# A linear-attention and two-layer kernel: the rows of its two split heads moved by four transfers instead of twelve

## The chip, the core and the metric

The kernel runs on one core of a Trainium2 chip. A core has a matrix engine (TensorE, PE in the profile, with its weight loads as PEld), three engines for elementwise work (VectorE or DVE, ScalarE or ACT, GpSimd or POOL), and a queue (SyncE, SP) on which this kernel issues all its transfers to 16 DMA engines. Each engine works through its own list of instructions in order and waits at an instruction until what it needs is there. The metric is the device time of one execution in microseconds (us); less is better.

## The reference

Gated linear attention over 4 batches, 8 heads, 768 steps and 48 features a head, then two feed-forward layers over the 3072 tokens (`d_model` 384, `d_ff` 2048 and 1536):

```python
state = np.zeros((B, H, D, D))
for t in range(S):
    state = alpha[:, :, t, :, None] * state + einsum('bhd,bhe->bhde', k[:, :, t], v[:, :, t])
    y[:, :, t] = einsum('bhd,bhde->bhe', q[:, :, t], state)
x = y.transpose(0, 2, 1, 3).reshape(B * S, H * D)
h = x @ w_in;  x = (h * np.cos(h)) @ w_out          # first layer
out = ((x @ w_a) * (x @ w_b)) @ w_out2              # second layer
```

## The kernel before

**Units.** The attention is cut into 48 units of 64 steps (12 for each batch). A unit has its input (`in_t`, for the first eight units `w_t`), two scans on DVE over the gates (L288, L300, with a reciprocal L297 between), products with queries and keys on POOL or DVE (L312, L325), a transpose and the scores on PE (L358, L368, L371), a copy of the transposed keys on ACT (`kn`, L363), the masked scores on DVE (`m`, L397 or L404), the new state and the outputs on PE (L430 to L450), and the state's decay (L499, or L514 and L517). The outputs of a unit leave PSUM twice: ACT rounds them (L547), DVE takes the rest that the rounding left (L550). These two, hi and lo, are the first layer's input, so that three products of rounded numbers stand for one product of full ones.

**The layer's input.** A group is 512 tokens, or eight units. Its input is two tiles, `xhi_t` and `xlo_t`, of 128 partitions x 4 slots x 512 columns. A unit writes partitions 0 to 47 (an even head) and 64 to 111 (an odd head) of all four slots. The layer reads only slots 0 to 2, as three blocks of 128 features; so heads 6 and 7, which stand in slot 3, have to come to the free partitions 48 to 63 and 112 to 127 of the slots 0 to 2. Once for every four units (12 times in all) SP issues transfers inside SBUF that do this: `move`, L563 to L573. The order of the rows of `w_in` (`perm`, L1084) follows from where the rows go.

**The layers.** A step of the first layer is nine 128x512 products into `hp` (L647), a cosine made by ACT and DVE in turn (L697, L700, L705), the product with `h` (L708), its rounding and rest (L712, L716), and nine products into `acc` (L654). There are 16 steps for each of 6 groups. For the first group the first two steps are done in halves of 256 columns: the first half needs the first move (units 0 to 3), the second half the second move (units 4 to 7). The second layer has 12 steps for each group (`ap`, `bp`, `acc`).

**Weights** come as 64-bit floats: 34 transfers `st_t<-wts` (L586) of 768 KB into three buffers. ACT scales the upper word (L590) and, for the first 16, makes the lower bits (L595; later L597 on DVE), DVE puts the bits together (L601, L607; the last of them frees the buffer for a later transfer), ACT rounds (L616), POOL takes the rest (L627).

**The order.** Every piece of work above is given to `Plan` with an engine, a duration in us, a lag (time from its end until others see it), what it needs and sometimes a due time. `Plan.run` simulates the five engines with these numbers and emits the instructions in the order in which that simulation starts them. So a duration in such a call changes no instruction, but can change the order on every engine. Around the place of the change:

```python
ops["ld"] = op(SP, 1.75, load, lag=2.0)      # a unit's input
mv = op(SP, 0.8, move, E["yx", k4], lag=2.0) # the transfers of four units
ld = op(SP, 2.4, load, after, lag=2.0)       # a weight pair
us = ou = op(PE, 2.0 + (0.8 if carry else 0.0), block, ...)
```

Of the kernel before, what the change touches and what calls it, by code (L numbers as in the profile page):

```python
# [28 lines left out]
P = 128  # L29
# [137 lines left out]
def chunked(ctx: ExitStack, tc: tile.TileContext, u_in: bass.AP, wts: bass.AP, out: bass.AP, in_range: bass.AP):  # L167
# [86 lines left out]

    def xtile(g):
        if g not in xg:
            xg[g] = tuple(xpool.tile([P, NP, G], F32R, name=f"x{n}_t") for n in ("hi", "lo"))
        return xg[g]

    def plan_load(u):  # L260
        d, ops = un[u], U[u]
        if "ld" in ops:
            return ops["ld"]
        def load():
            if u < UG:
                t = wpool.tile([P, 2, 2 * DM], F32R, name="w_t").bitcast(F32)
                d["in"] = t.rearrange("p a c -> p (a c)")[:, 0:IN_COLS]
            else:
                d["in"] = att.tile([P, IN_COLS], F32, name="in_t", bufs=NIN)
            cuts = (0, NA + 1, IN_COLS) if u == 0 else (0, IN_COLS)  # L270
            for c0, c1 in zip(cuts, cuts[1:]):
                nc.sync.dma_start(out=d["in"][:, c0:c1], in_=u_in[u, :, c0:c1])  # L272

        ops["ld"] = op(SP, 1.75, load, lag=2.0)
        ops["in_last"] = take("w_t", NPAIR1, ops["ld"]) if u < UG else take("in", NIN, ops["ld"])
        return ops["ld"]

    def plan_front(u):
        d, ops = un[u], U[u]
        apart = u < APART  # L280
        due = unit_due(u)

        ld, in_last = plan_load(u), U[u]["in_last"]

        def scan_a():
            d["ar"] = att.tile([112, 2, NP, SEP], F32, name="ar_t", bufs=NAR)
            d["a"], d["r"] = d["ar"][:, 0], d["ar"][:, 1]
            nc.vector.tensor_tensor_scan(  # L288
                d["a"].rearrange("p c t -> p (c t)"), d["in"][0:112, 0:NA], first.rearrange("p c t -> p (c t)"), 0.0,
                op0=ALU.mult, op1=ALU.add,  # L290
            )

        sa = op(DVE, 0.7, scan_a, [ld], port=True)
        ar_last = take("ar", NAR, sa)

        def recip():
            nc.vector.reciprocal(last[:, :, C:SEP], d["a"][:, :, C:SEP])  # L297

        def scan_r():
            nc.vector.tensor_tensor_scan(  # L300
                d["r"].rearrange("p c t -> p (c t)")[:, ::-1], d["in"][0:112, NA:0:-1],
                last.rearrange("p c t -> p (c t)")[:, ::-1], 0.0, op0=ALU.mult, op1=ALU.add,
            )

        rc = op(DVE, 0.18, recip, [sa, U[u - 1]["sr"] if u else None])
        sr = ops["sr"] = op(DVE, 0.7, scan_r, [rc], port=True)
        m = m_t[u % 3]
        m_before = U[u - 3]["ou"] if u >= 3 else []
        ma = [
            op(  # L310
                POOL, 0.73,
                lambda rows=rows, i=i: nc.gpsimd.tensor_tensor(  # L312
                    m[rows, i + apart], part(u, 0)[rows], d["a"][rows, :, 1:], op=ALU.mult
                ),
                [sa, *m_before], port=True,
            )
            for rows, i in HEADS
        ]
        kt = k_t[u % 2]
        k_before = U[u - 2]["k_last"] if u >= 2 else []  # L320
        on = DVE if u < UG else POOL
        eng = nc.vector if on == DVE else nc.gpsimd
        k = [op(
            on, 0.45 if on == DVE else 0.75,
            lambda: eng.tensor_tensor(kt, d["r"][:, :, 1:], part(u, 1), op=ALU.mult), [sr, *k_before], port=True,  # L325
        )]

        def in_range_sum():
            nc.scalar.activation(  # L329
                d["in"][0:112, W_A - 2 * NA:W_A], d["ar"].rearrange("p a c t -> p (a c t)"), AF.Square,  # L330
                accum_out=ranges[:, u:u + 1],
            )

        rg = op(ACT, 0.82, in_range_sum, [sr, *ma, *k], due=due + 2.0)
        E.setdefault("ranges", []).append(rg)
        in_last += [rg]
        ar_last += [rg, *ma, *k]

        ops.update(k=k, ma=ma, in_last=in_last, ar_last=ar_last, m_before=m_before)
# [4 lines left out]
    def plan_scores(u, block=None):  # L344
# [44 lines left out]
        ops["emit"] = ([transpose] if state else []) + [score]  # L389
        ops["k_last"] = [sc]  # L390
        if state:
            ops["kn"] = kn = op(ACT, 0.36, copy_k, [sc, *(U[u - 2]["us_op"] if u >= 2 else [])])
            ops["tu"] += [kn]
        if apart:
            mk = [op(
# [18 lines left out]
    def plan_back(u):  # L414
# [56 lines left out]
        else:  # L471
# [9 lines left out]
                if state and carry:  # L481
                    old_state()

            us = ou = op(PE, 2.0 + (0.8 if carry else 0.0), block, [kn, ld, *mk, *ma, *before], due=due)
            tu_last, sy_last = take("tu", 1, us), take("sy", 1, us)
            ops["us_op"] = [us]
            if u + 1 < NU:
# [64 lines left out]
                op0=ALU.mult, op1=ALU.subtract,  # L552
            )

        xh = op(ACT, 0.46, hi, [ou])
        if off == 0:
            E["xl", g] = take("x", 2, xh)
            E["xfirst", g] = xh
        need(xh, E["xfirst", g] if off else None)
        xl = op(DVE, 0.44, lo, [xh])  # L560
        sy_last += [xh, xl]
        E.setdefault(("yx", k4), []).extend([xh, xl])
        if off4 == UB - 1:  # L563
            def move():
                xc = slice((k4 % 2) * XB, (k4 % 2 + 1) * XB)
                xs = [t.bitcast(F32) for t in xg[g]]
                for n in range(2):
                    for r0 in (0, 64):
                        for j in range(KT):
                            nc.sync.dma_start(  # L570
                                out=xs[n][r0 + 48:r0 + 64, j, xc], in_=xs[n][r0 + 16 * j:r0 + 16 * j + 16, 3, xc]
                            )

            mv = op(SP, 0.8, move, E["yx", k4], lag=2.0)
            E["x", k4] = [mv, *E["yx", k4]]


# [5 lines left out]
    def plan_weights(i, after=(), gate=None):  # L583
# [42 lines left out]
            t = split.pop(i)  # L626
            nc.gpsimd.tensor_tensor(t[:, 1], conv.pop(i), t[:, 0].bitcast(F32), op=ALU.subtract)  # L627

        ld = op(SP, 2.4, load, after, lag=2.0)
        st_last = take("stage", NST, ld)  # L630
        s = op(ACT, 0.92, scale, [ld])
        wf_last = take("wf", 2, s)
# [2 lines left out]
        b1 = op(DVE, 0.93, bits1, [b0], port=True)  # L635
        h = op(ACT, 0.84, hi, [b1, gate])
        w_last = [] if NPAIR1 <= i < NPAIR1 + NLATE else take("w_t", NPAIR1, h)
        o = op(POOL, 1.95, lo, [h], port=True)
        st_last += [s, l, b0, b1]
        wf_last += [b0, b1, h, o]  # L640
        W[i] = dict(ld=ld, b1=b1, hi=h, lo=o, last=w_last)
# [25 lines left out]
    def plan_step(g, f):  # L667
# [3 lines left out]

        def mm():
            s["u"] = bank("hp", "hp", 3)
            by_k(s["u"], w1s[f, 0], *xg[g])

        def mm_part(n):
            def fn():
                if n == 0:
                    s["u"] = bank("hp", "hp", 3)
                by_k(s["u"][:, n * XB:(n + 1) * XB], w1s[f, 0], *(t[:, :, n * XB:(n + 1) * XB] for t in xg[g]))  # L680
            return fn

        w = [W[f]["hi"], W[f]["lo"]]
# [73 lines left out]
    def plan_x2(g):  # L757
# [4 lines left out]
        for j in range(KT):  # L762
            def hi(j=j):
                if j == 0:
                    x2s[g] = tuple(xpool.tile([P, NP, G], F32R, name=f"x{m}_t") for m in ("hi", "lo"))
                nc.scalar.copy(x2s[g][0][:, j, :], x2[g][:, j, :])  # L766

            def lo(j=j):
# [152 lines left out]
def step_by_step(  # L921
# [76 lines left out]
    with tc.For_i(0, NG, 1) as g:  # L998
        cols = bass.ds(g * G, G)
        x = pool.tile([P, KT, G], F32, name="g_x", bufs=1)  # L1000
        for j in range(KT):
            for r0, f0, n in (
                (0, 2 * j * D, D), (48, 6 * D + 16 * j, 16), (64, (2 * j + 1) * D, D), (112, 7 * D + 16 * j, 16)
            ):
                nc.sync.dma_start(out=x[r0:r0 + n, j, :], in_=y_all[f0:f0 + n, cols])
        nc.vector.tensor_scalar(x, x, XS, None, op0=ALU.mult)
        accs = [bank(f"g_acc{j}") for j in range(KT)]
        for f in range(NF1):
# [104 lines left out]
```

## Time and profile before

| | |
|---|---|
| time, median of 3 runs | 996.8 us (994.27 to 997.29) |
| profiled execution | 997.82 us, of it the span of the trace 996.0 us |
| PE busy | 975.5 us (98%), 6909 matrix products |
| PEld, DVE, ACT, POOL busy | 799.5, 524.9, 407.8, 227.7 us |
| mean granted clock of PE | 0.988 of full speed |
| chain that ended last | PE 90%, DMA 3%, SPq 2%, ACT 2%, DVE 1% |

The span is what lies between the first and the last instruction of the trace. Times of rows are counted from its start. "SPq" is the time in which SP issues transfers; what the transfers themselves take is told separately as the time to landing. A granted clock of 1.00 is 2.4 GHz and of 0.50 is 1.2 GHz; a mean between them says for how much of a stretch each was granted. An idle time stands in square brackets behind the instruction that ended it, with what released it.

### The profile page before, as it was taken

Reading aid. Unit: us, or ns where it says so; the run is one execution under the profiler, and the core shown is the slowest. Engines: PE = TensorE matmul, PEld = TensorE weight load, DVE = VectorE, ACT = ScalarE, POOL = GpSimd, SP = SyncE. Lnnn points to the kernel's source line nnn. Section 1 sums busy time; section 2 is a strip of 40 time slices with the busy share of each in tenths; the row PEclk is TensorE's granted clock in tenths of the full one; section 3 lists DMA queues with packets and bytes.
Section 4 is the critical chain, followed back from the end, with each engine's and each line's share of the span. In section 5 each row is a group of like instructions: output and inputs, shape, how many; then the busy total and the mean of one; then the engine's idle time right before and its main releaser. Section 6 shows DMA issues by size and latency. Waiting matters only on the chain.

```text
span 996.0 us, 16910 instructions
## 1 busy us (share of the span) xinstructions
PE 975.5 (98%) x6909; PEld 799.5 (80%) x6909; DVE 524.9 (53%) x887; ACT 407.8 (41%) x754; POOL 227.7 (23%) x259
## 2 busy tenths in 40 slices
PE   8799999999999999999999999999999999999997
PEld 6588788888888888888788888888888888888885
DVE  8689787766666766765777862222222222222221
ACT  4377765445454444543766542212222212112111
POOL 4546552323332231320323431001001001000000
PEclk9889999999999999999999999999999999999999
DMA  9344512211221221210432310000000000000000
GB/s 357 106 165 176 186 37 69 81 57 50 80 76 34 74 76 32 73 33 11 175 109 96 127 64 1 32 1 0 33 1 1 32 1 1 32 1 13 20 1 35
DMA packets 19237, 63.40 MB, mean 64 GB/s; under 512 B 3920, under 2 KB 6352, under 8 KB 19152
## 3 DMA queue, kind: packets, MB, share of 16 engines
q1 hardware_dynamic: 19152, 62.24, 18.0%
q8 instruction: 56, 0.92, 0.4%
q14 instruction: 29, 0.24, 0.1%
HBM read 55.15 MB, written 4.72 MB: 60 GB/s over the span
## 4 chain that ended last, share of the span: by engine, by line
PE 90%; DMA 3%; SPq 2%; ACT 2%; DVE 1%; issue 1%; DVEq 0%; ACTq 0%
PE acc L654 33%; PE hp L647 18%; PE bp L647 15%; PE ap L647 15%; DMA st_t<-wts 3%; PE sy L446 2%; PE tu L358 2%; SPq L570 2%; PE sy L368 2%; PE tu L431 1%; PE tu L430 1%; SPq L272 0%; ACT st_t L595 0%; PE sy L450 0%; PE tu L434 0%
## 5 line engine op out<-in xcount | busy, mean ns | idle before, releaser
L654 PE MATMUL acc<-ghi_t,w_t 128*128 128x512 f32 x972 | 302.2, 392 | 2.3 <-ACT ghi_t L712 2.3
L654 PEld LDWEIGHTS acc<-ghi_t,w_t 128*128 128x128 f32 x972 | 182.3, 188 | 41.2 <-ACT ghi_t L712 3.2
L654 PE MATMUL acc<-glo_t,w_t 128*128 128x512 f32 x486 | 190.5, 392 | 1.2 <-DVE glo_t L716 1.2
L809 DVE TENSOR_TENSOR bp<-c_t,bp 128x512 f32<-128x512 f32 x72 | 50.1, 696 | 264.1 <-PE bp L647 235.4
L647 PE MATMUL hp<-xhi_t,w_t 128*128 128x512 f32 (+1 forms) x588 | 153.2, 396 | 4.6 <-ACT in_t L329 3.9
L647 PEld LDWEIGHTS hp<-xhi_t,w_t 128*128 128x128 f32 x588 | 108.6, 191 | 28.0 <-ACT w_t L616 4.1
L806 ACT COPY c_t<-ap 128x512 f32<-128x512 f32 x72 | 42.3, 587 | 179.0 <-PE ap L647 178.9
L654 PEld LDWEIGHTS acc<-glo_t,w_t 128*128 128x128 f32 x486 | 91.6, 188 | 22.1 <-DVE glo_t L716 2.7
L647 PE MATMUL bp<-xhi_t,w_t 128*128 128x512 f32 x396 | 100.6, 389 | 0.0
L813 ACT CAST ghi_t<-bp 128x512 fp32r<-128x512 f32 x72 | 42.3, 588 | 141.8 <-DVE bp L809 141.8
L647 PE MATMUL ap<-xhi_t,w_t 128*128 128x512 f32 x360 | 91.4, 389 | 0.0
L697 ACT ACTIVATE c_t<-hp 128x512 int32<-128x512 f32 x96 | 57.5, 599 | 71.8 <-PE hp L647 71.3
L647 PEld LDWEIGHTS bp<-xhi_t,w_t 128*128 128x128 f32 x396 | 74.3, 188 | 15.7
L700 DVE CUSTOM_DVE_ANT_0 c_t<-c_t,hp 128x512 f32<-128x512 int32 x96 | 65.8, 685 | 38.6 <-ACT c_t L697 38.3
L627 POOL TENSOR_TENSOR w_t<-wf_t,w_t 128x768 fp32r<-128x768 f32 x32 | 64.4, 2015 | 94.0 <-ACT w_t L616 93.8
L647 PE MATMUL hp<-xlo_t,w_t 128*128 128x512 f32 (+1 forms) x294 | 83.2, 390 | 0.9 <-DMA xlo_t<-xlo_t 0.8
L769 POOL TENSOR_TENSOR xlo_t<-x,xhi_t 128x512 fp32r<-128x512 f32 x18 | 24.3, 1376 | 260.0 <-ACT xhi_t L766 167.7
L712 ACT CAST ghi_t<-hp 128x512 fp32r<-128x512 f32 x96 | 56.2, 586 | 55.4 <-DVE hp L708 54.7
L647 PEld LDWEIGHTS ap<-xhi_t,w_t 128*128 128x128 f32 x360 | 67.6, 188 | 14.1
L708 DVE TENSOR_TENSOR hp<-c_t,hp 128x512 f32<-128x512 f32 x96 | 66.0, 688 | 22.2 <-ACT c_t L705 21.3
L705 ACT ACTIVATE c_t<-c_t 128x512 f32<-128x512 f32 x96 | 60.5, 630 | 38.6 <-DVE c_t L700 37.4
L325 POOL TENSOR_TENSOR k<-ar_t,in_t 112x256 f32<-112x256 f32 x40 | 31.3, 781 | 192.7 <-PE sy L371 145.9
(120 smaller groups left out, 1380.6 us busy)
## 6 DMA issues: line engine op xcount, KB each, us to landing
st_t<-wts SPq DMA_DIRECT2D x34, 768.0 KB, 4.3
in_t<-u_in SPq DMA_DIRECT2D x40, 578.0 KB, 3.7
out<-o_t SPq DMA_DIRECT2D x18, 256.0 KB, 2.3
w_t<-u_in SPq DMA_DIRECT2D x7, 578.0 KB, 7.6
xhi_t<-xhi_t SPq DMA_DIRECT2D x72, 16.0 KB, 2.3
xlo_t<-xlo_t SPq DMA_DIRECT2D x72, 16.0 KB, 1.8
w_t<-u_in SPq DMA_DIRECT2D x1, 447.5 KB, 3.5
w_t<-u_in SPq DMA_DIRECT2D x1, 130.5 KB, 2.1
```

The lines of the kernel that those rows point to most:

```text
L325: lambda: eng.tensor_tensor(kt, d["r"][:, :, 1:], part(u, 1), op=ALU.mult), [sr, *k_before], port=True,
L627: nc.gpsimd.tensor_tensor(t[:, 1], conv.pop(i), t[:, 0].bitcast(F32), op=ALU.subtract)
L647: nc.tensor.matmul(acc, wt[:, w, j * P:(j + 1) * P], r[:, j, :], start=i == 0, stop=i == len(terms) - 1)
L654: nc.tensor.matmul(accs[j], wt[:, w, j * P:(j + 1) * P], r, start=first and i == 0, stop=last and i == 2)
L697: nc.scalar.activation(s["c"].bitcast(I32), s["u"], AF.Identity, bias=-0.25, scale=-1.0)
L700: nc.vector._custom_dve(TENSOR_ADD_SAT, out=s["c"], in0=s["c"].bitcast(I32), in1=s["u"], s0=0.25, s1=-0.75)
L705: nc.scalar.activation(s["c"], s["c"], AF.Sin, bias=math.pi / 2, scale=TWO_PI)
L708: nc.vector.tensor_tensor(s["u"], s["c"], s["u"], op=ALU.mult)
L712: nc.scalar.copy(s["hi"], s["u"])
L806: nc.scalar.copy(s["c"], s["a"])
L809: nc.vector.tensor_tensor(s["b"], s["c"], s["b"], op=ALU.mult)
L813: nc.scalar.copy(s["hi"], s["b"])
```

## The change

Hi and lo of the layer's input become one tile, `x_t`, of 128 partitions x 2 x 4 slots x 512 columns; the second layer's input too. A move is then four transfers, one for each of hi and lo and of the two heads: each takes 48 partitions of slot 3 and writes 16 partitions x 3 slots, in 256 columns (48 KB instead of 16 KB). Row 3p + s of a split head goes to partition p of slot s, where before it was row 16s + p; `perm` and the fallback path follow. In the calls of `Plan` some durations and lags are changed, among them that of the move (0.8 to 2.6, lag 2.0 to 1.5), of the loads and of the attention's block on PE.

```diff
@@ -254,7 +254,8 @@
 
     def xtile(g):
         if g not in xg:
-            xg[g] = tuple(xpool.tile([P, NP, G], F32R, name=f"x{n}_t") for n in ("hi", "lo"))
+            t = xpool.tile([P, 2, NP, G], F32R, name="x_t")
+            xg[g] = t[:, 0], t[:, 1], t
         return xg[g]
 
     def plan_load(u):
@@ -271,7 +272,7 @@
             for c0, c1 in zip(cuts, cuts[1:]):
                 nc.sync.dma_start(out=d["in"][:, c0:c1], in_=u_in[u, :, c0:c1])
 
-        ops["ld"] = op(SP, 1.75, load, lag=2.0)
+        ops["ld"] = op(SP, 1.5, load, lag=1.7)
         ops["in_last"] = take("w_t", NPAIR1, ops["ld"]) if u < UG else take("in", NIN, ops["ld"])
         return ops["ld"]
 
@@ -308,7 +309,7 @@
         m_before = U[u - 3]["ou"] if u >= 3 else []
         ma = [
             op(
-                POOL, 0.73,
+                POOL, 0.7,
                 lambda rows=rows, i=i: nc.gpsimd.tensor_tensor(
                     m[rows, i + apart], part(u, 0)[rows], d["a"][rows, :, 1:], op=ALU.mult
                 ),
@@ -331,7 +332,7 @@
                 accum_out=ranges[:, u:u + 1],
             )
 
-        rg = op(ACT, 0.82, in_range_sum, [sr, *ma, *k], due=due + 2.0)
+        rg = op(ACT, 0.85, in_range_sum, [sr, *ma, *k], due=due + 2.0)
         E.setdefault("ranges", []).append(rg)
         in_last += [rg]
         ar_last += [rg, *ma, *k]
...
@@ -481,7 +482,7 @@
                 if state and carry:
                     old_state()
 
-            us = ou = op(PE, 2.0 + (0.8 if carry else 0.0), block, [kn, ld, *mk, *ma, *before], due=due)
+            us = ou = op(PE, 2.35 + (0.8 if carry else 0.0), block, [kn, ld, *mk, *ma, *before], due=due)
             tu_last, sy_last = take("tu", 1, us), take("sy", 1, us)
             ops["us_op"] = [us]
             if u + 1 < NU:
@@ -552,26 +553,23 @@
                 op0=ALU.mult, op1=ALU.subtract,
             )
 
-        xh = op(ACT, 0.46, hi, [ou])
+        xh = op(ACT, 0.4, hi, [ou])
         if off == 0:
             E["xl", g] = take("x", 2, xh)
             E["xfirst", g] = xh
         need(xh, E["xfirst", g] if off else None)
-        xl = op(DVE, 0.44, lo, [xh])
+        xl = op(DVE, 0.42, lo, [xh])
         sy_last += [xh, xl]
         E.setdefault(("yx", k4), []).extend([xh, xl])
         if off4 == UB - 1:
             def move():
                 xc = slice((k4 % 2) * XB, (k4 % 2 + 1) * XB)
-                xs = [t.bitcast(F32) for t in xg[g]]
-                for n in range(2):
-                    for r0 in (0, 64):
-                        for j in range(KT):
-                            nc.sync.dma_start(
-                                out=xs[n][r0 + 48:r0 + 64, j, xc], in_=xs[n][r0 + 16 * j:r0 + 16 * j + 16, 3, xc]
-                            )
-
-            mv = op(SP, 0.8, move, E["yx", k4], lag=2.0)
+                t = xg[g][2].bitcast(F32)
+                for r0 in (0, 64):
+                    for n in range(2):
+                        nc.sync.dma_start(out=t[r0 + 48:r0 + 64, n, 0:KT, xc], in_=t[r0:r0 + 48, n, 3, xc])
+
+            mv = op(SP, 2.6, move, E["yx", k4], lag=1.5)
             E["x", k4] = [mv, *E["yx", k4]]
 
 
...
@@ -635,7 +633,7 @@
         b1 = op(DVE, 0.93, bits1, [b0], port=True)
         h = op(ACT, 0.84, hi, [b1, gate])
         w_last = [] if NPAIR1 <= i < NPAIR1 + NLATE else take("w_t", NPAIR1, h)
-        o = op(POOL, 1.95, lo, [h], port=True)
+        o = op(POOL, 1.88, lo, [h], port=True)
         st_last += [s, l, b0, b1]
         wf_last += [b0, b1, h, o]
         W[i] = dict(ld=ld, b1=b1, hi=h, lo=o, last=w_last)
@@ -671,13 +669,13 @@
 
         def mm():
             s["u"] = bank("hp", "hp", 3)
-            by_k(s["u"], w1s[f, 0], *xg[g])
+            by_k(s["u"], w1s[f, 0], *xg[g][0:2])
 
         def mm_part(n):
             def fn():
                 if n == 0:
                     s["u"] = bank("hp", "hp", 3)
-                by_k(s["u"][:, n * XB:(n + 1) * XB], w1s[f, 0], *(t[:, :, n * XB:(n + 1) * XB] for t in xg[g]))
+                by_k(s["u"][:, n * XB:(n + 1) * XB], w1s[f, 0], *(t[:, :, n * XB:(n + 1) * XB] for t in xg[g][0:2]))
             return fn
 
         w = [W[f]["hi"], W[f]["lo"]]
...
@@ -1082,7 +1082,7 @@
 
     rows = np.arange(DM).reshape(H, D)
     perm = np.stack([
-        np.concatenate([rows[2 * j], rows[6, 16 * j:16 * j + 16], rows[2 * j + 1], rows[7, 16 * j:16 * j + 16]])
+        np.concatenate([rows[2 * j], rows[6, j::KT], rows[2 * j + 1], rows[7, j::KT]])
         for j in range(KT)
     ])
     plain = np.arange(DM).reshape(KT, P)
```

Names in the new kernel lie one to three lines elsewhere (L570 is still the move, L272 becomes L273, L586 becomes L584). No instruction other than the moves is added or taken away, but they stand in another order at many places. Three of them follow.

On SP, around the first two moves (a row with x6 is six instructions), before:

```order
L272 DMA in_t<-u_in 128x1156
L570 DMA xhi_t<-xhi_t 16x256 x6
L570 DMA xlo_t<-xlo_t 16x256 x6
L272 DMA in_t<-u_in 128x1156
L586 DMA st_t<-wts 128x768
L570 DMA xhi_t<-xhi_t 16x256 x6
L570 DMA xlo_t<-xlo_t 16x256 x6
L586 DMA st_t<-wts 128x768 x2
```

and now:

```order
L273 DMA in_t<-u_in 128x1156 x2
L570 DMA x_t<-x_t 16x3x256 x4
L584 DMA st_t<-wts 128x768
L570 DMA x_t<-x_t 16x3x256 x4
L584 DMA st_t<-wts 128x768 x2
```

Beside the smaller number, the input of unit 11 now stands ahead of the first move instead of behind it.

On DVE, behind the last rest of units 4 to 7 (L550, now L551) and up to the masked scores of unit 8 (`m2`), before (`wf_t_374` and `wf_t_660` are the second and third weight pair, `ar_t_606` and `ar_t_676` the scans of units 8 and 9):

```order
L300 SCALAR_TENSOR_TENSOR ar_t_606<-in_t_351,last_91 112x260
L288 SCALAR_TENSOR_TENSOR ar_t_676<-in_t_362,first_90 112x260
L607 SCALAR_TENSOR_TENSOR wf_t_374<-st_t_297,wf_t_374 128x768
L297 RECIPROCAL last_91<-ar_t_676 112x4
L300 SCALAR_TENSOR_TENSOR ar_t_676<-in_t_362,last_91 112x260
L601 SCALAR_TENSOR_TENSOR wf_t_660<-wf_t_660,st_t_397 128x768
L397 TENSOR_TENSOR m2_101<-sy_697,mask_95 128x256
```

and now (`wf_t_365` and `wf_t_649` are these two weight pairs):

```order
L301 SCALAR_TENSOR_TENSOR ar_t_611<-in_t_309,last_91 112x260
L599 SCALAR_TENSOR_TENSOR wf_t_365<-wf_t_365,st_t_271 128x768
L289 SCALAR_TENSOR_TENSOR ar_t_658<-in_t_334,first_90 112x260
L605 SCALAR_TENSOR_TENSOR wf_t_365<-st_t_271,wf_t_365 128x768
L298 RECIPROCAL last_91<-ar_t_658 112x4
L301 SCALAR_TENSOR_TENSOR ar_t_658<-in_t_334,last_91 112x260
L599 SCALAR_TENSOR_TENSOR wf_t_649<-wf_t_649,st_t_359 128x768
L605 SCALAR_TENSOR_TENSOR wf_t_649<-st_t_359,wf_t_649 128x768
L698 ISA c_t_678<-c_t_678,hp_639 128x512
L289 SCALAR_TENSOR_TENSOR ar_t_687<-in_t_397,first_90 112x260
L298 RECIPROCAL last_91<-ar_t_687 112x4
L398 TENSOR_TENSOR m2_101<-sy_690,mask_95 128x256
```

The first of the second pair's two operations (L601 before, L599 now) stood ahead of the last rests of units 6 and 7 and now stands behind them; and the second operation of the third pair, the first cosine's L698 and the first scan of unit 10 with its reciprocal have come ahead of the masked scores of unit 8.

On ACT, in the first step of the first layer, before:

```order
L697 ACTIVATE c_t_715<-hp_650 128x512
L363 COPY kn0_109<-tu_696 128x4x48
L705 ACTIVATE c_t_715<-c_t_715 128x512
L595 ACTIVATE st_t_683<-st_t_683 128x768
L616 CAST w_t_731<-wf_t_660 128x768
L712 CAST ghi_t_778<-hp_650 128x512
```

and now:

```order
L695 ACTIVATE c_t_678<-hp_639 128x512
L614 CAST w_t_683<-wf_t_649 128x768
L330 ACTIVATE in_t_309,ranges_113<-ar_t_611 112x520
L364 COPY kn0_109<-tu_689 128x4x48
L703 ACTIVATE c_t_678<-c_t_678 128x512
L593 ACTIVATE st_t_665<-st_t_665 128x768
L593 ACTIVATE st_t_685<-st_t_685 128x768
L710 CAST ghi_t_766<-hp_639 128x512
```

Two operations on two newly loaded weight pairs (L593) now stand together ahead of the rounding of the first step's result (`ghi`), where one stood.

## Rows read from the trace of the kernel before

**Rows 1.** Busy time by stretch: us, then busy us of PE, PEld, DVE, ACT, POOL; PEclk; DMA

```profile
36.40:58.20 21.80, 15.74 (x151) 13.51 (x151) 13.19 (x24) 9.82 (x18) 12.09 (x10) 0.61 0.39 131
98.00:112.00 14.00, 11.53 (x110) 9.18 (x111) 8.82 (x16) 8.89 (x15) 6.19 (x5) 0.88 0.57 217
112.00:458.00 346.00, 346.00 (x3252) 284.97 (x3251) 242.30 (x463) 172.90 (x350) 108.61 (x161) 1.00 0.20 62
458.00:485.00 27.00, 25.85 (x124) 20.19 (x123) 13.92 (x22) 13.89 (x24) 6.38 (x4) 1.00 0.33 117
```

**Rows 2.** PE in order of time, second half of the first step: start, us, instruction

```profile
45.54 1.75 PE L647 MATMUL hp<-xlo_t,w_t 128*128 128x256 f32 x3 [0.84 <-DMA xlo_t<-xlo_t]
...
49.72 0.47 PE L446 MATMUL sy<-m,in_t 112*64 112x64 f32 x4 [0.53 <-DVE m L397]
```

**Rows 3.** SP in order of time, around the second move

```profile
37.89 3.67 SPq L570 DMA_DIRECT2D xhi_t<-xhi_t  x6
41.61 3.82 SPq L570 DMA_DIRECT2D xlo_t<-xlo_t  x6
45.52 0.53 SPq L586 DMA_DIRECT2D st_t<-wts  x1
```

**Rows 4.** Line L570, issue of one transfer: ns least/median/most, first and last start

```profile
L570 SPq DMA_DIRECT2D xhi_t<-xhi_t x72: 507/587/1322, 24.0 to 466.8; - x72
```

**Rows 5.** Line L586, the same for the weights' transfers

```profile
L586 SPq DMA_DIRECT2D st_t<-wts x34: 327/328/633, 5.2 to 577.6; - x34
```

**Rows 6.** Part 6 of the page, issues: KB each, median us to landing

```profile
xhi_t<-xhi_t SPq DMA_DIRECT2D x72, 16.0 KB, 2.3
xlo_t<-xlo_t SPq DMA_DIRECT2D x72, 16.0 KB, 1.8
```

**Rows 7.** DVE in order of time, from unit 7 to the masked scores of unit 8

```profile
34.42 2.51 DVE L601 SCALAR_TENSOR_TENSOR wf_t<-wf_t,st_t 128x768 int32<-128x768 int32 x1
...
37.45 0.41 DVE L550 SCALAR_TENSOR_TENSOR xlo_t<-acc,xhi_t 112x256 fp32r<-112x256 f32 x1
...
49.24 0.43 DVE L397 TENSOR_TENSOR m<-sy,mask 128x256 f32<-128x256 f32 x1 [7.38 <-PE sy L371]
```

**Rows 8.** Groups of instructions by line: count, busy us, mean ns, idle before

```profile
L700 DVE CUSTOM_DVE_ANT_0 c_t<-c_t,hp 128x512 f32<-128x512 int32 x96 | 65.8, 685 | 38.6 <-ACT c_t L697 38.3
...
L601 DVE SCALAR_TENSOR_TENSOR wf_t<-wf_t,st_t 128x768 int32<-128x768 int32 x34 | 36.6, 1077 | 0.6
L607 DVE SCALAR_TENSOR_TENSOR wf_t<-st_t,wf_t 128x768 int32<-128x768 int32 x34 | 35.9, 1057 | 0.3
...
L288 DVE TENSOR_TENSOR_SCAN ar_t<-in_t,first 112x260 f32<-112x260 f32 x40 | 28.6, 716 | 25.0 <-DMA in_t<-u_in 25.0
```

**Rows 9.** ACT in order of time, start-up, unit 3

```profile
17.98 0.90 ACT L590 ACTIVATE wf_t<-st_t 128x768 f32<-128x768 f32 x1
18.78 0.30 ACT L363 COPY kn<-acc 128x192 f32<-128x192 f32 x1
```

**Rows 10.** Chain that ended last, in order of time: start, us, what

```profile
5.18 12.77 DMA st_t<-wts
...
96.31 8.29 DMA st_t<-wts
```

**Rows 11.** SP in order of time, around the third move

```profile
87.32 4.00 SPq L570 DMA_DIRECT2D xhi_t<-xhi_t  x6
...
95.21 0.53 SPq L586 DMA_DIRECT2D st_t<-wts  x1
```

**Rows 12.** ACT in order of time, behind the third move

```profile
104.62 0.90 ACT L595 ACTIVATE st_t<-st_t 128x768 int32<-128x768 uint16 x1 [2.40 <-DMA st_t<-wts]
```

**Rows 13.** PE in order of time, behind the third move

```profile
107.81 0.73 PE L654 MATMUL acc<-ghi_t,w_t 128*128 128x512 f32 x2 [2.35 <-ACT ghi_t L712]
```

**Rows 14.** DVE in order of time, behind the last move

```profile
476.50 0.56 DVE L597 TENSOR_SCALAR st_t<-st_t 128x768 int32<-128x768 int32 x1 [5.53 <-DMA st_t<-wts]
```

**Rows 15.** PE in order of time, behind the last move

```profile
477.71 0.50 PE L654 MATMUL acc<-glo_t,w_t 128*128 128x512 f32 x1 [0.94 <-DVE glo_t L716]
```

More of the change, by code (lines that the diff above doesn't have):

```diff
@@ L391, in plan_scores @@
         if state:
-            ops["kn"] = kn = op(ACT, 0.36, copy_k, [sc, *(U[u - 2]["us_op"] if u >= 2 else [])])
+            ops["kn"] = kn = op(ACT, 0.34, copy_k, [sc, *(U[u - 2]["us_op"] if u >= 2 else [])])
             ops["tu"] += [kn]
@@ L627, in lo @@
             nc.gpsimd.tensor_tensor(t[:, 1], conv.pop(i), t[:, 0].bitcast(F32), op=ALU.subtract)
-        ld = op(SP, 2.4, load, after, lag=2.0)
+        ld = op(SP, 2.0, load, after, lag=1.8)
         st_last = take("stage", NST, ld)
@@ L764, in hi @@
                 if j == 0:
-                    x2s[g] = tuple(xpool.tile([P, NP, G], F32R, name=f"x{m}_t") for m in ("hi", "lo"))
+                    t = xpool.tile([P, 2, NP, G], F32R, name="x_t")
+                    x2s[g] = t[:, 0], t[:, 1]
                 nc.scalar.copy(x2s[g][0][:, j, :], x2[g][:, j, :])
@@ L1002, in step_by_step @@
             for r0, f0, n in (
-                (0, 2 * j * D, D), (48, 6 * D + 16 * j, 16), (64, (2 * j + 1) * D, D), (112, 7 * D + 16 * j, 16)
+                (0, 2 * j * D, D), (48, 6 * D + j, 16), (64, (2 * j + 1) * D, D), (112, 7 * D + j, 16)
             ):
-                nc.sync.dma_start(out=x[r0:r0 + n, j, :], in_=y_all[f0:f0 + n, cols])
+                step = KT if n == 16 else 1
+                nc.sync.dma_start(out=x[r0:r0 + n, j, :], in_=y_all[f0:f0 + (n - 1) * step + 1:step, cols])
         nc.vector.tensor_scalar(x, x, XS, None, op0=ALU.mult)
```

## The prediction

> **What bounds the kernel now.** I read the stretches first, then PE's waits inside them, then the queue that these waits lead to. For 346 us in the middle PE is never idle, and its granted clock is 1.00 [rows 1]; eight of the twelve moves lie there, so nothing that they save can shorten that stretch. What a move can be worth is in three places. From 36.4 to 58.2 us PE is busy for 15.74 of 21.8 us at a mean clock of 0.61: (1 - 0.61) / 0.5 x 21.8 = 17 us of it at 1.2 GHz. From 98 to 112 it is idle for 2.47 us, at a mean clock of 0.88, which is 3.4 us at 1.2 GHz. From 458 to 485 it is idle for 1.15 us [rows 1]. The reader is to see that a move ends just ahead of each of the three.
>
> **First place, the second move.** PE does the second half of the layer's first step with the rows that this move brings. Its last three products start at 45.54, released by the transfer of lo, and end at 45.54 + 1.75 = 47.29 [rows 2]. Until then PE's list stands, and with it the transpose and scores of unit 8, whose result DVE's masking waits for: 7.38 us, up to 49.24 [rows 7]. PE's next output work starts at 49.72 [rows 2]. The move's twelve issues run from 37.89, when the rest of unit 7 has ended (37.45 + 0.41 = 37.86 [rows 7]), to 41.61 + 3.82 = 45.43 [rows 3]: 7.5 us for twelve, 0.63 each with the gap, of which 0.587 is the issue [rows 4]. The issue, not the landing (median 1.8 to 2.3 us [rows 6]), is what takes the time.
>
> The Trainium skill says otherwise: issuing from several engines "will only save the time on the sequencer it takes to initiate the DMA, which is usually small relative to the DMA itself" (DMA: Bandwidth & Descriptors, "Issuing engines are not separate DMA queues"). By that rule fewer issues would save next to nothing and the sum would be 996.8; here twelve issues take 7.5 us against 1.8 to 2.3 of landing, so the rows go against it and I follow the rows.
>
> What four transfers of 48 KB cost to issue, no row shows. A 768 KB transfer is issued in 0.327 us, a 16 KB one in 0.587 [rows 4, 5]: bytes don't set it. The low end is 0.33; the high end is growth with the rows that are taken (48 for 16), 3 x 0.587 = 1.76. I take 0.59, the row of the same kind of transfer, so 4 x 0.63 = 2.5 us for a move. For the landing I take 2.3, the upper of the two medians, since the transfer is larger.
>
> Where does the move start? Two edits of the order bear on it. ACT's scaling of the first weight pair now stands ahead of three operations and of unit 3's `kn`, and waits for a transfer that lands at 5.18 + 12.77 = 17.95 [rows 10]. Before, `kn` started at 18.78, behind that scaling alone [rows 9]; now three more lie between, at most 0.90 each by the scaling's row [rows 9], so up to 2.7 us late. On the other side, L601 of the second pair, which took 2.51 us ahead of the rests of units 6 and 7 [rows 7], now stands behind them. 2.7 - 2.5 = 0.2 us late is what I take, so the move starts at 38.1; the ends are 2.5 early and 2.7 late. That the input of unit 11 is issued ahead of the first move costs 0.33 [rows 5] at a time when nobody waits for that move.
>
> The fourth issue starts 3 x 0.63 = 1.9 us after 38.1, lands at 42.3, and PE is through with its last three products by about 43.0, for 47.29: 4.3 us earlier. Transpose and scores of unit 8 took from 47.29 to 49.24, 2.0 us at 1.2 GHz [rows 2, 7]; that ends at 45.0. But DVE is late next. Behind unit 7's rest it did six instructions before its wait, from 37.86 to 49.24 - 7.38 = 41.86: 4.0 us [rows 7]. Now there are also L601 (1.08), L607 (1.06), the first cosine's L700 (0.69) and a scan L288 (0.72) ahead of the masking [rows 8], and a reciprocal of some 0.2: 3.7 us. So masking starts at 38.1 + 4.0 + 3.7 = 45.8, ends at 46.2, and PE's output work starts then, for 49.72. **First term: 3.5 us.** Its low end comes from the issue at 1.76: last start 5.3 us after 38.1, landing 45.7, scores 48.4, output work 48.9, so 0.8 us. Its high end adds the clock. I let PE run at 1.2 GHz as long as before, since it still pauses twice; if the shorter pauses kept it at 2.4 GHz, the work from 49.72 to 58.2 would take half of its 8.5 us: 4.2 more.
>
> **Second place, the third move.** It holds SP from 87.32 to 95.16; the weight transfer behind it starts at 95.21 [rows 11], and the next one at 96.31 takes 8.29 us to land, because it shares the engines with it [rows 10]. ACT waits 2.40 us for that one at 104.62 [rows 12], and has the rounding behind it for which PE waits 2.35 us [rows 13]; then PE runs 3.4 us at 1.2 GHz, which costs 1.7 us. With four issues the queue is free at 87.3 + 2.5 = 89.8, up to 5.4 us sooner, more than ACT's wait. All of it would be 2.35 + 1.7 = 4.0. The order of ACT and DVE is a new one here, so some of it may come back as another wait: between 0 and 4.0 I take 3.0. **Second term: 3.0 us.**
>
> **Third place, the last move.** The first weight of the second layer is issued behind it. DVE stands 5.53 us at that weight (L597) [rows 14], with the rest (`glo`) behind it for which PE waits 0.94 us [rows 15]. The new order has that rest ahead of the weight's operation, and the weight comes 5.4 us sooner. **Third term: 1.1 us** of the 1.15 that PE is idle there [rows 1]; ends 0 and 1.15.
>
> The eight moves under the 346 us, the single tile (same size, same readers) and the new order of `w_in` cost nothing: PE's work covers the moves, and where PE is never idle for 346 us a change of order on the other engines shows only if one of them falls behind; DVE, the fullest, is busy for 242 of 346 [rows 1].
>
> **Sum.** 3.5 + 3.0 + 1.1 = 7.6 us off the profiled execution's 997.8: 990.2. That execution is 1.0 us over the median of the runs; against the median it is 989.2.
>
> **Rivals.**
> *An issue grows with the rows it takes* (1.76 us each). For it: nothing shows what sets 0.587 against 0.327. Against: 128 rows are issued in 0.327 [rows 5]. A move then lasts 7.2 us instead of 7.8: 0.8 + 0.5 + 0.2 = 1.5 off, 995.3. 8 in 100.
> *The gain is taken back by the new order before 112 us.* For it: DVE, ACT and PE are all well filled there, and `kn` of unit 3 may be 2.7 us late with nothing returned. The first term is then 3.5 - 2.5 = 1.0, and the second 0: 2.1 off with the third, 994.7. Against it: the 7.38 us in which DVE stood [rows 7] are room enough. 10 in 100.
> *Slower: the two weight operations (L593) that now stand together on ACT.* They are ahead of the first step's `ghi`. The second needs a transfer whose buffer is free only when L605 of the third pair is done, by the sum above at about 44.2; until it has landed ACT stands, and `ghi`, `glo` and PE's first `acc` with it. PE would want that `acc` at 58.2 - 3.5 = 54.7. With a landing of 8.29 us [rows 10] ACT goes on at 52.5 and `ghi` and `glo` are there at about 54.7: that is the point from which it decides. With the start-up's 12.77 [rows 10] `acc` comes 4.5 us late, 1.0 more than the first term gave; the order has one more such pair in the first group, for 4.5 again, and the second term doesn't come: 996.8 + 1.0 + 4.5 - 1.1 = 1001.2. Against it: the queue is emptier than at the start. 8 in 100.
>
> **How the numbers follow.** The forecast has 74 in 100. A measurement can tell about 0.3%, 3.0 us, from no change: faster is below 993.8, slower above 999.8. Faster has the forecast and a share of the first two rivals' spread, 0.76; the same 0.16; slower 0.08. The range goes down to all terms in full and the clock, 4.2 + 3.5 + 4.0 + 1.15 = 12.9 off, 983.9, and up to the first rival, 995.5; what is left out is the slower case and the rest of the order's spread.
>
> **What would show it.** L570 with 48 issues, near 0.6 us each (the first rival: 1.8). The second half of the first step done near 43 and the outputs of unit 8 near 46.2; DVE's 7.38 us gone and PE, not DVE, idle for some 1 to 2 us ahead of the masking. No PE wait near 107 and a clock of 1.00 there; no weight wait of 5.5 us on DVE behind the last move. A `kn` of unit 3 near 21 shows the start-up's delay. The prediction is wrong if ACT waits for weights ahead of `ghi`, or if the stretch between the first group's end and 990 changes its length.

## The result, and the profile after

The changed kernel takes 988.87 us (median of 5 runs, 988.28 to 989.68), the kernel before beside it 997.2 us (994.27 to 999.61): a ratio of 0.9907, 95% interval 0.9887 to 0.9928. The profiled execution is the one of 988.87 us, span 987.2 us, for 997.8 and 996.0 before.

To read single profiles one thing has to be known: in the first 36 us the granted clock falls for some us in ten of the fourteen profiled executions here, three of them with the old order on every engine (last section), and what follows comes up to 5 us later. So a place is measured from its own start, not on absolute times.

I read the gain with a ruler: the start of PE's n-th product with a step's second weights (`acc`), before minus after. This lead is 2.0 us at the first one (58.24 before, 56.29 after) and stays so to 93 us; it is 7.0 at 117, 7.1 from 143 to 476, and 9.5 from 491 to the last product. Behind that 0.6 us go again: from the start of the last such product to the end of the trace it is 7.8 us for 7.3, which leaves the span's 8.9. So the time comes from the three places of the prediction: 2.0, 5.0 (and 0.1) and 2.3.

The stretches after, with the columns of [rows 1] (length, busy times of PE, PEld, DVE, ACT and POOL with their instructions, granted clock):
```profile
36.40:55.00 18.60, 14.84 (x184) 13.26 (x180) 16.84 (x23) 10.01 (x18) 14.88 (x12) 0.64 0.47 157
98.00:112.00 14.00, 14.00 (x141) 11.78 (x137) 12.18 (x19) 10.47 (x18) 8.63 (x5) 1.00 0.53 191
112.00:450.00 338.00, 338.00 (x3149) 278.43 (x3149) 237.04 (x455) 167.96 (x342) 106.13 (x158) 1.00 0.19 60
450.00:478.00 28.00, 28.00 (x138) 22.96 (x137) 18.56 (x27) 16.61 (x31) 6.42 (x4) 1.00 0.33 120
```
The second and third places of [rows 1] are full and at 2.4 GHz. The first is not: PE still runs (1 - 0.64) / 0.5 x 18.6 = 13 us at 1.2 GHz. The moves themselves, in the view of their line (ns, minimum, median, maximum) and on SP's queue:
```profile
L570 SPq DMA_DIRECT2D x_t<-x_t x48: 556/585/1277, 26.1 to 458.4; - x48
DMA to landing us min/median/max: 2.2/2.5/5.1
```
```profile
39.28 2.47 SPq L570 DMA_DIRECT2D x_t<-x_t  x4
42.69 0.33 SPq L584 DMA_DIRECT2D st_t<-wts  x1
...
82.48 3.03 SPq L570 DMA_DIRECT2D x_t<-x_t  x4
86.52 0.33 SPq L584 DMA_DIRECT2D st_t<-wts  x1
```
An issue of 48 rows costs what one of 16 cost, 0.585 us for 0.587 [rows 4], and the queue is held 2.47 us instead of 7.5 [rows 3]. What PE and DVE make of it at the second move:
```profile
38.48 1.34 PE L645 MATMUL hp<-x_t,w_t 128*128 128x256 f32 x9
42.88 2.26 PE L645 MATMUL hp<-x_t,w_t 128*128 128x256 f32 x9 [3.05 <-DMA x_t<-x_t]
47.75 0.48 PE L447 MATMUL sy<-m,in_t 112*64 112x64 f32 x4 [0.71 <-DVE m L398]
56.29 0.63 PE L652 MATMUL acc<-ghi_t,w_t 128*128 128x512 f32 x2
```
```profile
38.83 0.42 DVE L551 SCALAR_TENSOR_TENSOR x_t<-acc,x_t 112x256 fp32r<-112x256 f32 x1 [1.07 <-ACT x_t L548]
...
47.30 0.40 DVE L398 TENSOR_TENSOR m<-sy,mask 128x256 f32<-128x256 f32 x1
47.62 4.17 DVE L301 TENSOR_TENSOR_SCAN ar_t<-in_t,last 112x260 f32<-112x260 f32 x1
```
DVE's 7.38 us [rows 7] are gone: it masks unit 8 without having waited, and PE waits 0.71 for DVE.

### The profile page after: what moved, and what is told of

Read it like the earlier page. It is cut to its first block, busy times and chain, and to the rows that moved or that the text cites. A ratio compares the mean times of both kernels' runs of the same rounds, so it can differ in the third digit from the quotient of the medians.

```text
span 987.2 us, 16801 instructions
## 1 busy us (share of the span) xinstructions
PE 972.0 (98%) x6909; PEld 800.6 (81%) x6909; DVE 529.3 (54%) x887; ACT 407.6 (41%) x754; POOL 230.9 (23%) x259
## 4 chain that ended last, share of the span: by engine, by line
PE 95%; DMA 2%; DVE 1%; SPq 0%; issue 0%; ACT 0%
PE acc L652 35%; PE hp L645 20%; PE bp L645 15%; PE ap L645 15%; PE sy L447 3%; PE tu L359 2%; PE sy L369 2%; DMA st_t<-wts 2%; PE tu L432 1%; DMA w_t<-u_in 1%; PE tu L431 1%; PE sy L451 0%; PE tu L435 0%; DVE wf_t L605 0%; DVE wf_t L599 0%; PE sy L372 0%
## 5 line engine op out<-in xcount | busy, mean ns | idle before, releaser
L645 PE MATMUL hp<-x_t,w_t 128*128 128x512 f32 (+1 forms) x882 | 217.9, 392 | 3.1 <-DMA x_t<-x_t 3.1
L645 PEld LDWEIGHTS hp<-x_t,w_t 128*128 128x128 f32 x882 | 163.3, 191 | 37.0 <-issue 3.5
L645 PE MATMUL bp<-x_t,w_t 128*128 128x512 f32 x594 | 145.6, 389 | 0.0
L645 PE MATMUL ap<-x_t,w_t 128*128 128x512 f32 x540 | 132.2, 389 | 0.0
L645 PEld LDWEIGHTS bp<-x_t,w_t 128*128 128x128 f32 x594 | 111.5, 188 | 23.5
L645 PEld LDWEIGHTS ap<-x_t,w_t 128*128 128x128 f32 x540 | 101.4, 188 | 21.2
L768 POOL TENSOR_TENSOR x_t<-x,x_t 128x512 fp32r<-128x512 f32 x18 | 25.1, 1416 | 256.9 <-ACT x_t L765 256.9
L698 DVE CUSTOM_DVE_ANT_0 c_t<-c_t,hp 128x512 f32<-128x512 int32 x96 | 65.6, 683 | 25.3 <-ACT c_t L695 24.9
L714 DVE TENSOR_TENSOR glo_t<-hp,ghi_t 128x512 fp32r<-128x512 f32 x96 | 65.4, 681 | 18.4 <-ACT ghi_t L710 18.2
```

What stands on the lines that cost most here:

```text
L645: nc.tensor.matmul(acc, wt[:, w, j * P:(j + 1) * P], r[:, j, :], start=i == 0, stop=i == len(terms) - 1)
L698: nc.vector._custom_dve(TENSOR_ADD_SAT, out=s["c"], in0=s["c"].bitcast(I32), in1=s["u"], s0=0.25, s1=-0.75)
L714: nc.vector.tensor_tensor(s["lo"], s["u"], s["hi"].bitcast(F32), op=ALU.subtract)
```

## The experiments

**Order and transfers apart.** Theory: the time of the issues made the gain. Rival: the new order made it. Two kernels complete the square (old and new order, each with twelve and with four transfers): the old order, instruction for instruction on all five engines, with four transfers, and the new order with twelve.
`old_order_4` is the changed kernel with all the planner's numbers as before, as in the first two lines; `new_order_12` has the other lines.
```diff
-            mv = op(SP, 2.6, move, E["yx", k4], lag=1.5)
+            mv = op(SP, 0.8, move, E["yx", k4], lag=2.0)
...
-                        nc.sync.dma_start(out=t[r0 + 48:r0 + 64, n, 0:KT, xc], in_=t[r0:r0 + 48, n, 3, xc])
+                        for j in range(KT):
+                            nc.sync.dma_start(out=t[r0 + 48:r0 + 64, n, j, xc], in_=t[r0 + j:r0 + 48:KT, n, 3, xc])
```


> The order of the kernel before on all five engines, instruction for instruction, with four transfers for a move instead of twelve. Theory (the issues of the moves cost the time, the new order is worth little): the second move starts at 37.9 as before, PE's second half starts 3.6 us behind it as in the changed kernel, 41.5, and PE's output work at 46.2 for 49.72, 3.5 us; behind the third move the 5.0 us and behind the last the 2.3 us of the changed kernel come as well: 10.8 off the 997, about 986 to 988. Rival 1 (the new order makes the gain): 996 to 998. Rival 2 (both halves are needed, since the old order has DVE at the weight ahead of the rest behind the last move): 990 to 992.

> The changed kernel's order with twelve transfers for every move (16 rows each, every third row of the 48). Theory: the gains at the three places go back, 9.5 us of lead at the end of PE's work: 997 to 999. Rival 1 (the new order makes the gain): 989. Rival 2 (the new order does worse than the old one with long moves, since it plans a move of 2.6 us): 1000 to 1004, with waits behind moves in the stretch that was full.

> The changed kernel as it is, for the comparison on one chip with the three others. Both theories: 0.990 to 0.992 of the kernel before, 988 to 991.

> The order of the kernel before with four transfers for a move, once more, for the comparison on one chip with the two others and for a second profile. Theory: 988 to 989, PE idle in the second half's wait and at 1.2 GHz behind it; from the start of the second move to the end of the masking 7.8 to 8.3 us, as in its first profile and the changed kernel's.

| time over that of the kernel before (95%) | twelve | four |
|---|---|---|
| old order | 1 | 0.9889 (0.9871 to 0.9907), again 0.9896 (0.9875 to 0.9917) |
| new order | 0.9975 (0.9962 to 0.9988) | 0.9907 (0.9887 to 0.9928), again 0.9916 (0.9894 to 0.9937) |

The transfers carry it: alone they give all that the change gives, 988.71 and 988.91 us, though the expected 986 to 988 was a little too low. The new order alone is worth 2.4 us (996.33, below the expected 997 to 999), which I had not expected, and beside short moves nothing that these times can tell. In its one profile the place is the third move, over which the lead grows by 3.1: twelve issues still make PE wait there, but for 1.9 us and with the clock at 1.00, for 0.88 in [rows 1]:
```profile
98.00:112.00 14.00, 12.10 (x122) 9.85 (x120) 10.17 (x17) 10.84 (x20) 7.95 (x5) 1.00 0.55 189
```

**One place at a time.** The twelve issues are put back in one move alone: k4 == 1 in `second_12`, 2 in `third_12` (and `old_third_12`, on the old order), 11 in `last_12`, 3 to 10 in `mid_12`.
```diff
+                if k4 == 1:
+                    for n in range(2):
+                        for r0 in (0, 64):
+                            for j in range(KT):
+                                nc.sync.dma_start(
+                                    out=t[r0 + 48:r0 + 64, n, j, xc], in_=t[r0 + j:r0 + 48:KT, n, 3, xc]
+                                )
+                    return
```


> The changed kernel with twelve transfers in the second move alone. Theory: the move then lasts from 39.3 to 46.8, PE's second half ends at 48.9, scores at 50.8, output work starts at 51.3 for 47.75, 3.5 us later; PE's lead at the first product with the second weights of the step (56.3) shrinks by 2.0 to 3.5, and the time is 990.9 to 992.4. Rival (DVE, which is busy without a gap from 39 to 56 us, sets the place and not the move): under 0.8, 989 to 989.7.

0.9948 (0.9929 to 0.9967), 994.26 us: 3 to 4 us over the changed kernel by the ratios, about 5.5 by the medians, and above the expected 990.9 to 992.4. The place in this kernel's trace:
```profile
38.63 7.49 SPq L572 DMA_DIRECT2D x_t<-x_t  x12
```
```profile
42.36 2.49 PE L653 MATMUL hp<-x_t,w_t 128*128 128x256 f32 x6 [3.19 <-DMA x_t<-x_t]
46.27 1.67 PE L653 MATMUL hp<-x_t,w_t 128*128 128x256 f32 x3 [1.43 <-DMA x_t<-x_t]
```
```profile
50.03 0.40 DVE L398 TENSOR_TENSOR m<-sy,mask 128x256 f32<-128x256 f32 x1
```
From the start of the move to the masking it is 11.40 us, as before (49.24 - 37.89 = 11.35 [rows 3, 7]), against 8.02 with four: 3.4 us, as expected at this place. The rival, that DVE sets the place whatever the move does, falls: it sets it only once the move is short (`warm_new` below).

> The changed kernel with twelve transfers in the third move alone. Theory: weights come later behind it, ACT waits, PE waits 2.4 us near 105 and runs some 4 us at 1.2 GHz: 5.0 us back, 993 to 994.5. Rival (the new order of ACT and DVE covers the late weights): no PE wait there, under 0.8 us, 989 to 989.7.

> The order of the kernel before with four transfers for a move and twelve in the third move alone. Theory: ACT waits over 2 us for the weight behind the move, PE waits about 2.3 near 105 and runs at 1.2 GHz behind it, as in the kernel before; 4.2 to 4.5 us slower than this order with four everywhere (988.8): 993. Rival (what the third move costs at its place is made good in the time of the whole, as the time of the changed kernel with twelve there might mean): within 1.5 of 988.8, 0.989 to 0.991 of the kernel before.

In the new order the times say little: 0.9911 (0.9893 to 0.9929), 990.76 us, below the expected 993 to 994.5, and by the ratio it can't be told from the changed kernel. The trace says more: the lead over this place grows by 1.2 us instead of 5.0. ACT stands at a weight behind the move, DVE behind ACT, and PE behind DVE:
```profile
93.92 0.90 ACT L601 ACTIVATE st_t<-st_t 128x768 int32<-128x768 uint16 x1 [4.66 <-DMA st_t<-wts]
```
```profile
95.37 0.70 DVE L714 TENSOR_TENSOR hp<-c_t,hp 128x512 f32<-128x512 f32 x1 [3.16 <-ACT c_t L711]
95.97 0.42 DVE L551 SCALAR_TENSOR_TENSOR x_t<-sy,x_t 112x256 fp32r<-112x256 f32 x1
```
```profile
96.49 0.33 PE L447 MATMUL sy<-m,in_t 112*64 112x64 f32 x4 [2.26 <-issue]
```
PE's row names no releaser. That it waits for DVE's L551, which reads `sy` and ends at 96.39, is inferred from the order. So the wait came, 10 us earlier than expected. In the old order time and trace agree: 0.9931 (0.991 to 0.9952), 991.61 us, 3.5 to 4.2 us over that order's 0.9889 and 0.9896 (2.7 to 2.9 by the medians; 993 was expected). The lead grows by 0.5 there instead of 4.5 and 4.2, and the waits of [rows 12, 13] are back:
```profile
102.75 0.90 ACT L601 ACTIVATE st_t<-st_t 128x768 int32<-128x768 uint16 x1 [2.09 <-DMA st_t<-wts]
```
```profile
105.95 0.73 PE L660 MATMUL acc<-ghi_t,w_t 128*128 128x512 f32 x2 [2.05 <-ACT ghi_t L718]
```

> The changed kernel with twelve transfers in the last move alone. Theory: the first weight of the second layer comes 5 us later, ACT and DVE stand at it and PE waits for ghi or glo near 470, 2.3 to 2.9 us slower than the changed kernel. Rival (the new order, which has the rest ahead of the weight's operation on DVE, covers the late weight): within 0.5 of the changed kernel.

0.9959 (0.994 to 0.9978), 992.9 us, for 988.71 of the changed kernel beside it. At the place the lead falls by 0.8 where it grew by 2.3, 3.1 us in all. What PE and its weight loads (PEld) wait for from 455 to 490 (total, times, longest):
```profile
PEld acc L660 <- ACT ghi_t L718: 1.7, 1, 1.7
PEld acc L660 <- DVE glo_t L722: 1.5, 2, 1.0
PE acc L660 <- ACT ghi_t L718: 1.2, 1, 1.2
PE acc L660 <- DVE glo_t L722: 0.5, 1, 0.5
```
The new order of the rest doesn't cover a late weight: ACT's scaling (L596) stands 5.3 us at it, and the rounding (`ghi`) behind. The medians differ by 1 us more than this. Three of twelve runs were at 996 to 997, the profiled one among them, but without them the median is still 992.7, so where this 1 us lies stays open; it is within the intervals.

> The changed kernel with twelve transfers in the fourth to eleventh moves, those under the stretch in which PE is never idle. Theory: they are hidden, within 0.5 of the changed kernel's 988.7, PE still without a gap from 112 to 450. Rival (a late weight behind one of these moves reaches PE, as behind the third move): a PE wait in that stretch, 2 to 4 slower.

0.9909 (0.9883 to 0.9934), 989.97 us where the kernel before took 999.66: by the ratio as expected, by the medians 1.3 us over the changed kernel. PE is idle for 0.6 us in the stretch that was to have no gap, and the lead falls there from 8.3 to 6.9 between 120 and 136 us, and then holds to 476. Half a microsecond of this lies ahead of the first long move (124.67); the other 0.9 goes in `second_12` too, which has four transfers in these moves. So the long moves are not shown to cost anything: the eight moves in the middle are hidden.

**Is it the clock that keeps the first place long?** Products on zeros fill PE's wait between the halves of the first step.
`warm_new` is the changed kernel with this edit, `warm_old` is `old_order_4` with it and 17 for 14. `keep_warm(n)` is a helper of the kernel that issues n such products.
```diff
                 if n == 0:
                     s["u"] = bank("hp", "hp", 3)
+                elif f == 0:
+                    keep_warm(14)
```


> The changed kernel with 14 products on zeros, whose result nobody reads, between the two halves of the layer's first step, where PE waits 3.1 us for the second move and runs at 1.2 GHz behind it. If the pause takes the clock: PE's clock from 40 to 55 rises from 0.6 to 1.0, the second half takes 1.3 for 2.3 us, and the stretch from PE's output work to the first product with the second weights, 8.5 us, shortens; DVE is busy there without a gap and ends the rest (glo) at 53.9, so 1 to 2.3 us faster than the changed kernel. Rival (the clock falls all the same, or DVE sets the place): no change within 0.5.

> The order of the kernel before with four transfers for a move, and 17 products on zeros, whose result nobody reads, between the two halves of the layer's first step. If the pause takes the clock: DVE has room here (it stood 3.9 us ahead of the masking), so masking comes about 2 us earlier and the 8 us behind it at 1.2 GHz halve: 3 to 5 us faster than this order without the products, 984 to 986. Rival (the clock falls all the same): no change within 0.5, 988 to 989.

PE's clock from 40 to 60 us is then 1.00 in both. In the new order it brings nothing: 0.9918 (0.9896 to 0.994), 988.89 us, for 988.71 of the changed kernel beside it. The rival holds, DVE sets the place: it masks unit 8 at 48.53, 8.02 us behind the start of the move (40.51) as without the products, and PE waits for DVE instead (46 to 100 us):
```profile
PE sy L447 <- DVE m L398: 2.5, 1, 2.5
PE acc L652 <- DVE glo_t L716: 1.1, 2, 0.8
```
In the old order, where DVE has room, it brings 3.3 us by the medians: 0.9881 (0.9857 to 0.9906), 985.46 us. By the ratios it is only 0.8 to 1.5 us, within the intervals; the next kernel is the clearer one.
```profile
41.30 3.86 PE L660 MATMUL acc<-zeros 128*64 128x512 bf16 x17
45.13 1.30 PE L645 MATMUL hp<-x_t,w_t 128*128 128x256 f32 x9
```
```profile
47.56 0.42 DVE L398 TENSOR_TENSOR m<-sy,mask 128x256 f32<-128x256 f32 x1 [2.07 <-PE sy L372]
```
The second half takes 1.30 us for 2.26. The move of this run started at 41.51, so masking comes after 6.05 us, for 7.81 (45.97 - 38.16) in `old_order_again`.

**The high parts first.** The loops over r0 and n in `move` change places, with 14 products on zeros.

> The order of the kernel before with four transfers for a move, the high parts of both heads first, and 14 products on zeros between the halves of the first step (17 without the new order of the four). Theory: the six products with high parts need the first two transfers alone, so the second half begins one issue, 0.6 us, sooner behind the start of the move (41.51 to 45.13, 3.6, becomes 3.0), masking and all behind it 0.6 sooner: about 0.6 under the kernel with 17, 984.9. Rival (landing, not issue, sets the start of the half): no change.

0.9853 (0.983 to 0.9877), 984.56 us, the fastest here and 4 us under the changed kernel. `old_order_again`, the same order without products and with the old sequence of the four, was run beside it: 988.25 to 990.48 us, for 984.03 to 986.35 here. So products and sequence together bring 4.3 us, clear of the noise. The step itself is half right:
```profile
41.03 0.94 PE L645 MATMUL hp<-x_t,w_t 128*128 128x256 f32 x6
42.25 0.59 PE L645 MATMUL hp<-x_t,w_t 128*128 128x256 f32 x3 [0.28 <-DVE wf_t L599]
```
The move starts at 38.07, so the half begins 2.96 us behind it for 3.62, as expected. But its last three products have to wait again, and masking comes after 5.90 for 6.05: 0.15 us. That they wait for the fourth transfer is inferred, since the row names an operation on a tile that they don't read. The rest of the difference of the two medians is within the intervals, so by this place nearly all of the 4.3 us is the products'.

## Why the prediction was right, and where it was not

**Start of the second move (38.1).** It started at 39.28, with `kn` of unit 3 at 22.01 (forecast near 21). A second profile of the changed kernel has 37.92 and 20.66. So the step was right. The profiled run's 1.2 us more I put down to the clock at the start, 0.66 from 10 to 20 us for 0.83 in the second profile.

**Issue and landing (4 x 0.63, 2.3).** 2.47 us for four, landing 2.5 in the median. Right, and with it the first rival (1.76 for an issue) falls. The rule of the Trainium skill (DMA: Bandwidth & Descriptors, "Issuing engines are not separate DMA queues") that issue time is usually small beside the transfer doesn't hold for these moves: in the old order 48 issues for 144 give 1.0 to 1.1%.

**The second half (4.9 us behind the move's start).** It ended 5.86 behind it. This step failed: I had only the last three products wait for the move's end. The third transfer brings the high part of the second head, so all nine wait for it, 3.6 us, and then take 2.26 at 1.2 GHz.

**DVE is late next (masking 7.7 behind the start).** 8.02 in both profiles of the changed kernel, without a wait, so the failed step cost nothing here. That was luck: another engine hid it. `warm_new` shows it: a faster PE gains nothing in this order. What I took for PE waiting 1 to 2 us was 0.71.

**First term, 3.5.** From the move's start to PE's output work 49.72 - 37.89 = 11.8 became 47.75 - 39.28 = 8.5: 3.4, and 3.4 by `second_12`. The lead of 2.0 is this less the late start. The high end, the clock kept at 2.4 GHz, did not come in the changed kernel's profiles (0.66 from 40 to 60 us in both); in that of `mid_12`, which is the changed kernel up to there, it is 0.91, and the gain counted from the move's start is no larger (last table).

**Second term, 3.0.** The lead grew by 5.0. The mechanism was the forecast one (no wait of ACT ahead of `ghi`, clock 1.00), the size was not: I had 4.0 for all of it and took a quarter off for the new order, which took nothing. The rest is a shorter wait of PE near 98 that also went (0.5) and that a wait costs a little more than PE's idle time in its row, 2.6 for 2.35. The transfers alone make 3.7 to 4.0 of it (`old_third_12`), and 3.9 in the new order (`third_12`).

**Third term, 1.1.** The lead grew by 2.3. I had sized it by PE's idle time [rows 1, 15], and that was the fault: a product that comes late because its weight load waited shows little idle time. The view of the waits of before, 440 to 500 us, had it:
```profile
PE acc L654 <- DVE glo_t L716: 1.2, 2, 0.9
```
```profile
PEld acc L654 <- DVE glo_t L716: 2.0, 2, 1.4
```
`last_12` confirms the place.

**No cost elsewhere.** Right for the eight moves (`mid_12`). The new order at nothing: right beside short moves, 2.4 us too little by itself. The second rival (the new order takes the gain back) falls with the square above; I can't tell the two orders with four transfers apart by their times. But its late `kn` is real and shows at the start of some runs (last section).

**The slower rival.** The pair of weight operations stands on ACT as told, and its second waits, but not long enough:
```profile
50.52 0.91 ACT L593 ACTIVATE st_t<-st_t 128x768 int32<-128x768 uint16 x1 [1.52 <-DMA st_t<-wts]
52.42 0.59 ACT L710 CAST ghi_t<-hp 128x512 fp32r<-128x512 f32 x1 [0.99 <-DVE hp L706]
```
ACT goes on at 50.5, below the 52.5 from which it would decide, and `ghi` then waits for DVE. By its words the sign that I had named for being wrong (ACT waits for weights ahead of `ghi`) did appear; it cost nothing, as PE has no wait for `ghi` there.

**Sum.** 7.6 forecast, 8.95 between the profiled executions, 8.3 between the medians. The time came out by errors of both signs, and that it came so close is in part luck: the first term 1.5 against (the late start), the second and third 3.3 for, the end behind the last product 0.6 against.

## What to carry to other kernels

Count the issues of a queue before its bytes: where a transfer is short, its place in the queue is paid in issues, and the first to pay may be a load behind it. Look for what stands next on the other engines before a wait is given up as gain, and size a wait of PE by its weight loads as well as by its idle time. A pause of PE ahead of a full stretch is paid twice, the second time in clock; work on zeros in the pause gives that back, but only where no other engine sets the pace.

## What the runs showed that I had not expected

**A scan on DVE stands still beside POOL.** Behind the masking of unit 8 the changed kernel's DVE has a scan (L301) that takes 4.17 us instead of 0.70. POOL, beside it:
```profile
47.62 3.62 POOL L625 TENSOR_TENSOR w_t<-wf_t,w_t 128x768 fp32r<-128x768 f32 x2
```
POOL ends at 51.24, the scan 0.55 us behind it, at 51.79. The fourteen traces together show the rule. Of their 1344 scans 1084 start while no elementwise operation of POOL runs, and take 0.70 us at most. The 260 others start while one runs: 233 of them end 0.55 to 0.56 us behind POOL's end, however long that takes, and 27, which start in its last 0.12 us, take 0.68 to 0.70. In five other profiles POOL's two operations stand without a gap beside this same scan, as here, and it takes 4.18 to 4.22. In `second_12`, with the same order on DVE and POOL, it meets only the last 1.2 us of one of them and takes 1.75:
```profile
49.37 2.17 POOL L633 TENSOR_TENSOR w_t<-wf_t,w_t 128x768 fp32r<-128x768 f32 x1 [0.98 <-DVE c_t L706]
```
```profile
50.35 1.75 DVE L301 TENSOR_TENSOR_SCAN ar_t<-in_t,last 112x260 f32<-112x260 f32 x1
```
So the scan waits for POOL. The Trainium skill (SBUF — State Buffer, "Who interferes with whom") has a rule for it: a DVE instruction with two inputs in SBUF contends with a GpSimd one that reads SBUF, and the ports that they share are an exclusive lock. The traces agree. Why DVE loses to two operations in a row, and not only to the first, stays open.

**The start scatters.** From 10 to 20 us the clock is 0.66 in the changed kernel's profile (first row) and 1.00 in that of `old_order_again` (second):
```profile
10.00:20.00 10.00, 9.69 (x160) 7.85 (x161) 6.72 (x16) 3.74 (x10) 3.41 (x4) 0.66 1.02 418
```
```profile
10.00:20.00 10.00, 9.65 (x232) 7.85 (x232) 8.83 (x21) 5.44 (x14) 4.63 (x6) 1.00 1.02 416
```
`old_third_12`, in the same order as the latter, has 0.66 too, and `last_12` 1.00 here but 0.58 from 20 to 36.4. Ahead of each fall PE had waited. In the seven profiles with less than 1.00 from 10 to 20 us, PE waits 1.13 to 1.87 us for DVE's masking near 10 us; in the seven others 1.08 or less. The fall behind 20 us comes in the new order alone, in three of the four profiles in which PE waits 1.7 to 2.5 us for unit 3's late `kn` (at most 0.5 in the old order), here in `warm_new`:
```profile
21.06 0.31 PE L431 MATMUL acc<-w_t,kn 64*48 64x48 f32 x1 [2.25 <-ACT kn L364]
```
That the waits set it off is argued and not shown, and why DVE's masking is late in some runs stays open.

Counted from the start of the second move to the last product with a step's second weights, the start drops out. By the one profile of each run this stretch is shorter than before (950.9 us) by:

| run | us |
|---|---|
| changed kernel, two profiles | 10.8, 10.4 |
| old order with four transfers, two profiles | 9.9, 9.7 |
| `new_order_12` | 2.5 |
| `second_12`, `third_12`, `last_12`, `mid_12` | 6.1, 6.8, 8.2, 10.8 |
| `old_third_12` | 7.2 |
| `warm_new`, `warm_old`, `warm_old_hi` | 11.6, 14.1, 14.8 |
